# Loading S1 and S2 on GpSimd's queue, keys and v on even and odd partitions, and another order, in a polysketch attention with an ELU block behind it

## The chip, the cores and the metric

One core of one Trainium2 chip. The metric is the device time of one execution in microseconds (us): the median of the runs, lower is better. Engines are named as in the profile: PE (TensorE, with PEld for its weight loads), DVE (VectorE), ACT (ScalarE), POOL (GpSimd) and SP (SyncE, which here only issues DMAs).

## The reference

Attention without a softmax: a key or query of 32 numbers is projected by S1 and by S2 to 8 numbers each, and the 64 products of the two are its features. The result then passes a block with two weight matrices and an ELU.

```python
# q, k, v: (4, 4, 1088, 32); S1, S2: (8, 32); w_in: (128, 2048); w_out: (2048, 128)
def phi(x):
    a = np.einsum('rd,bhsd->bhsr', S1, x)
    b = np.einsum('rd,bhsd->bhsr', S2, x)
    return np.einsum('bhsi,bhsj->bhsij', a, b).reshape(*x.shape[:-1], r * r)
q_p, k_p = (phi(q), phi(k))
kv = np.einsum('bhsf,bhsd->bhfd', k_p, v)
z = np.sum(k_p, axis=2)
num = np.einsum('bhsf,bhfd->bhsd', q_p, kv)
den = np.einsum('bhsf,bhf->bhs', q_p, z)[..., None] + 1e-06
# x = num / den, reordered to (4352, 128)
h = x @ w_in
g = np.where(h > 0.0, h, alpha * (np.exp(np.minimum(h, 0.0)) - 1.0))
return (g @ w_out).astype(np.float32)
```

S1, S2, w_in and w_out arrive as 64-bit floats; the kernel rounds them to 32 bits itself, with integer steps on the two words of each number.

## The kernel before

**Tiling.** A batch b has 1088 tokens, 17 tiles (NT) of 64. Keys and values are worked on two tiles at a time: u = 0 stands for tiles 0 to 8 (KT = 9), u = 1 for tiles 9 to 16, and partitions 0 to 63 of a 128-row tile belong to u = 0, 64 to 127 to u = 1. The u = 1 half of the ninth pair has no tile and is filled with zeros (L235 for v, L237 for kT). Queries go in groups g of 8 tiles; the hidden width of 2048 goes in 8 pairs cp of two 128-blocks c.

**The head** does batch 0. `load_hd` brings keys and queries to `hd`, `load_v` brings v; `transp` (L285, on DVE) turns keys to `kT` and queries to `qT`, with the 32 numbers of each of the 4 heads on 128 partitions. S1 and S2 land in `raw_s` (L164). DVE and POOL round them: strip (L127), low (L275, POOL), floor, shift, round_s (L119, DVE), then an add into `Sx` (L279, POOL). PE multiplies `Sx` with `ident` into `sps` (L305) and DVE masks that with `bmask` into `Sab` (L308), the weights of the features. `bmask`, `zmask` and `hmask` are three reduces of `ident` on DVE (L241 to L248); `ident` is made on POOL (masks.py). `KF_first` (L345) gives the features of the keys, one matmul for each 64-token tile and half u; `KF_first_out` (L354, ACT) copies them out in two parts. `KO_first` (L419, DVE) and `KO_pool` (L327, POOL) form the products of features; `KA_first` (L436) multiplies them with v; `Z_first`, `ZC`, `Z`, `Z_out` give the sum for the denominator; `KS_copy`, `KS_turn`, `KS_out` turn kv to `kvS`. On the query side there are `q1_first` (L524), `q1z_first` (L537), `q2_out` (L624), `q4_early` (L637, transposes on PE), `q1_second` (L546), `den_wide`, `den_turn`, `den_out` (L645 to L657), and `q5_early` with `q5_early_out` (L663, L675), which writes `xg`, the x of group 0. `mm1_first` multiplies its halves with the first block of w_in.

**The weights.** `load_w` issues 256 KB pieces on SP's queue; `R1(step, i)` is one rounding step of piece i of the list `order`: low (L142), strip (L127 on DVE, L129 on ACT), floor (L132), shift (L135), round_s (L119), whole (L145, POOL). Pieces 0 and 1 are w_in of cp 0 and 1, piece 2 is w_out of cp 0, and so on. `load_rest` issues everything beyond the first two pieces; a small memset on POOL (L221), behind `KO_pool`, stands ahead of it.

**The body.** For each group and pair: `mm1` (PE, h = w_in times xg), `elu_a` (ACT, L927 and L929), `elu_d` (DVE, L935, writes gg), and the product with w_out. For group 0 that is `mm2`; `mm2_blocks` does pair 0 of group 1; later pairs use `mm2_seven`, seven products in place of eight, which also needs `sums7` on POOL (L792 to L799) and `weights7`. h has four buffers in PSUM, e two and gg three. `KF_late`, `KO`, `KA`, `queries` and so on bring in batches 1 to 3 among these.

**The order.** Nothing is scheduled by a planner at build time: each engine and queue runs its instructions in the order in which the calls stand, from `zls = {}` on, in a list of 868 calls written out one by one. SP, ACT and POOL each have a DMA queue of their own; a DMA that waits holds what stands behind it on the same engine.

```python
for x, (eng, src) in enumerate(((nc.sync, S1), (nc.scalar, S2))):   # L161
for x, src, t0, t1 in (("k", k, 0, KT), ("k", k, KT, NT), ("q", q, 0, 8)):   # L167
    for c, eng in enumerate((nc.sync, nc.scalar)):
        load_hd(eng, x, src, 0, t0, t1, slice(c, c + 1))
load_v(0, (nc.sync, nc.scalar))
```

Of the kernel before, what the change touches and what calls it, by code (L numbers as in the profile page):

```python
# [12 lines left out]
F32 = mybir.dt.float32  # L13
# [16 lines left out]
def kernel(  # L30
# [21 lines left out]
    nc = tc.nc  # L52
# [21 lines left out]
    kT = [const.tile([FD, 2 * KT, 64], F32, name=f"kT{b}") for b in range(2)] * 2  # L74
    qT = [const.tile([FD, NT, 64], F32, name=f"qT{b}") for b in range(2)] * 2
    qE = const.tile([FD, 2, 64], F32, name="qE")

# [6 lines left out]
    def load_v(b, engs=(nc.sync, nc.sync)):  # L84
        for u, eng in enumerate(engs):
            t0, t1 = u * KT, min(NT, u * KT + KT)
            r = slice(64 * u, 64 * u + 64)
            src = v[b].rearrange("h (y t) d -> y h t d", t=NT)[:, :, t0:t1, :]
            eng.dma_start(vt[b][r, :VN].rearrange("p (h t d) -> p h t d", h=H, t=KT)[:, :, :t1 - t0, :], src)
# [67 lines left out]
    S16 = const.tile([2 * R, D], F32, name="S16")  # L157
    wide = S1.dtype != F32
    if wide:
        raw_s = const.tile([2 * R, D, 2], U32, name="raw_s")  # L160
    for x, (eng, src) in enumerate(((nc.sync, S1), (nc.scalar, S2))):  # L161
        rs = slice(R * x, R * x + R)
        if wide:
            eng.dma_start(raw_s[rs].rearrange("p c w -> p (c w)"), src.bitcast(U32))  # L164
        else:
            eng.dma_start(S16[rs, :], src)
# [67 lines left out]
    for b in range(B):  # L234
        nc.gpsimd.memset(vt[b][64:, :VN].rearrange("p (h t d) -> p h t d", h=H, t=KT)[:, :, KT - 1, :], 0.0)  # L235
        if b < 2:
            nc.gpsimd.memset(kT[b][:, NT:, :], 0.0)  # L237
# [46 lines left out]
    def transp(dst, x, b, t0, t1):  # L284
        nc.vector.transpose(dst[b][:, t0:t1, :].rearrange("p t (a c) -> p c t a", c=2), hd[x, b][:, :, t0:t1, :])  # L285
# [55 lines left out]
    def KF_first(*todo):  # L341
        if not kf_ps:
            kf_ps.extend(psum.tile([P, 512], F32, name="abp", tag="h", bufs=4) for _ in range(2))
        for i, u in todo:
            nc.tensor.matmul(kf_ps[i // 5][64 * u:64 * u + 64, 64 * (i % 5):64 * (i % 5) + 64],  # L345
                             kT[0][:, u * KT + i, :], Sab[:].rearrange("p h y -> p (h y)"),
                             skip_group_check=True, tile_position=(0, 64 * u))
# [9 lines left out]
    def KF_late(b, step=None):  # L357
# [4 lines left out]
        for c in range(4):  # L362
            u, w = divmod(c, 2)
            for g2 in range(2):
# [3 lines left out]
                                 kT[b][r, u * KT:u * KT + KT, 32 * w:32 * w + 32],  # L368
# [649 lines left out]

    transp(kT, "k", 0, 2, 5)
    KF_first((0, 0), (1, 0))  # L1020
    transp(kT, "k", 0, KT, KT + 5)
    KF_first((2, 0), (3, 0), (4, 0))
    KF_first((0, 1), (1, 1), (2, 1))
    transp(kT, "k", 0, 5, KT)
    KF_first((3, 1), (5, 0))
    KF_first((4, 1), (6, 0))
    KF_first_out(0)
    transp(kT, "k", 0, KT + 5, NT)
    transp(qT, "q", 0, 0, 8)
    KF_first((5, 1), (7, 0))  # L1030
    KF_first((6, 1), (8, 0))
    KF_first((7, 1), (8, 1))
    KF_first_out(1)
    KO_pool()
    load_rest()
    KO_first(4, 5)
    KO_first(5, 7)
    keep_warm(1, 96)
    Z_first(0, 1, 2, 3, 4)
    q1_first(0, 1)  # L1040
    q1_first(2, 3)
    Z_first(5, 6, 7, 8)
    zl = ZC(0, feats["z"])
    q1_first_out()
    q2_out(0, 1)
    Z(0, feats["z"], zl)
    KO_first(7, KT)
    Z_out(0, feats["z"])
    zq = q1z_first()
    q2_out(0, 0)  # L1050
    KA_first(range(4, KT), True, False)
    q2_prod(0, zq)
    KA_first(range(4), False, True)
    make_Sxp()
    q4_early(0, 0)
    transp(qT, "q", 0, 8, 13)
    q2_sum(0)
    transp(qT, "q", 0, 13, NT)
    R1(low, 0)
    R1(strip, 0, nc.scalar)  # L1060
    q2_rec(0)
    R1(strip, 1, nc.scalar)
    q4_early(0, 1)
    R1(floor, 0)
    R1(floor, 1)
    R1(shift, 0)
    R1(shift, 1)
    R1(round_s, 0)
    KS_copy()
    KS_turn()  # L1070
    abwp = q1_second()
    den_wide()
    q4_out(0, 0)
    KS_out()
# [3 lines left out]
    R1(round_s, 1)  # L1078
    q2_prod(1)
    den_out()  # L1080
    q5_early(0)
    q5_early_out(0, 0)
    q5_early_out(0, 1)
    R1(strip, 2, nc.scalar)
    whole_half(0, 1)
    whole_half(0, 0)
    mm1_first(0, (0,))
    mm1_first(0, (1,))
    mm1_first(1, (0, 1))
    R1(low, 1, nc.gpsimd)  # L1090
    q2_sum(1)
    q2_rec(1)
    q2_an(1)
    R1(low, 3)
    R1(low, 2)
    R1(strip, 3, nc.scalar)
    R1(whole, 1)
    mm1(0, 1, (1,))
    R1(strip, 4)
    q2_out(1, 1)  # L1100
    q2_out(1, 0)
    R1(floor, 4)
    R1(low, 4)
    elu_a(0, 0, 0, (0,))
    elu_a(0, 0, 0, (1,))
    R1(floor, 2)
    R1(shift, 4)
    R1(shift, 2)
    R1(round_s, 4)
    elu_a(0, 0, 1, (0,))  # L1110
    R1(whole, 4)
    R1(round_s, 2)
    R1(whole, 2)
    q4_early(1, 1)
    q4_out(1, 1)
    q4_early(1, 0)
    q4_out(1, 0)
    mm1(0, 1, (0,))
    elu_a(0, 0, 1, (1,))
    elu_d(0, 0, 0)  # L1120
    elu_d(0, 0, 1)
    KT_out(0)
    R1(floor, 3)
    R1(strip, 5)
    R1(floor, 5)
    q5_early(1)
    elu_a(0, 1, 0, (0,))
    elu_a(0, 1, 0, (1,))
    mm1(0, 2, (0,))
    elu_a(0, 1, 1, (0,))  # L1130
    R1(strip, 7)
    R1(shift, 3)
    R1(round_s, 3)
    elu_a(0, 1, 1, (1,))
    q5_early_out(1, 0)
    q5_early_out(1, 1)
    R1(whole, 3)
# [829 lines left out]
```

## Time and profile before

| | us |
|---|---|
| median of 3 runs | 259.7 (259.54 to 260.39) |
| the profiled execution | 259.92 |
| its span, from the first to the last instruction | 258.0 |
| first DMA issue on SP and ACT | 0.74 and 0.75 |
| first matmul of mm1_first | 15.68 |
| last large products end near | 254.5 |

Times in the profile count from the start of the span. Busy time is the time in which an engine has an instruction under way; a matmul's end is modelled. Behind each group stands in brackets the idle time of its engine just before it and what ended it. A group "x4" of a timeline is four instructions of one kind in a row, and its duration runs from the start of the first to the end of the last. "SPq" and "ACTq" are the sequencers of the two engines as they issue DMAs.

### The profile page before, as it was taken

Reading aid. Unit: us, or ns where it says so; the run is one execution under the profiler, and the core shown is the slowest. Engines: PE = TensorE matmul, PEld = TensorE weight load, DVE = VectorE, ACT = ScalarE, POOL = GpSimd, SP = SyncE. Lnnn points to the kernel's source line nnn. Section 1 sums busy time; section 2 is a strip of 40 time slices with the busy share of each in tenths; the row PEclk is TensorE's granted clock in tenths of the full one; section 3 lists DMA queues with packets and bytes.
Section 4 is the critical chain, followed back from the end, with each engine's and each line's share of the span. In section 5 each row is a group of like instructions: output and inputs, shape, how many; then the busy total and the mean of one; then the engine's idle time right before and its main releaser. Section 6 shows DMA issues by size and latency. Waiting matters only on the chain.

```text
span 258.0 us, 9832 instructions
## 1 busy us (share of the span) xinstructions
PE 252.2 (98%) x4135; PEld 160.6 (62%) x4135; DVE 175.1 (68%) x342; ACT 180.4 (70%) x355; POOL 185.3 (72%) x236
## 2 busy tenths in 40 slices
PE   8889999999999999999999999999999999999994
PEld 7752332436647667577566666667666666667994
DVE  5889999699879774889377965664265445644641
ACT  2589975857677757486568757776677777777792
POOL 5533457986996877877787889879589888888310
PEclk9999999999999999999999999999999999999999
DMA  6899866032100001210002042312101100110021
GB/s 189 239 286 276 276 176 173 4 102 47 27 5 4 3 10 38 32 24 3 3 10 31 5 89 33 86 33 36 20 1 21 23 3 0 22 27 0 3 31 33
DMA packets 30427, 15.61 MB, mean 60 GB/s; under 512 B 22544, under 2 KB 28048, under 8 KB 30384
## 3 DMA queue, kind: packets, MB, share of 16 engines
q1 hardware_dynamic: 29520, 14.22, 22.9%
q10 hardware_dynamic: 800, 0.71, 1.0%
q8 instruction: 32, 0.52, 0.9%
q14 instruction: 11, 0.09, 0.1%
q0 software_dynamic: 64, 0.07, 0.1%
HBM read 11.31 MB, written 2.36 MB: 53 GB/s over the span
## 4 chain that ended last, share of the span: by engine, by line
PE 98%; DVE 0%; issue 0%; ACT 0%; DVEq 0%
PE h L259 46%; PE pb L836 18%; PE pa L836 15%; PE o L259 5%; PE ol L259 3%; PE idle L267 2%; PE kv L450 1%; PE abp L345 1%; PE qtp L637 1%; PE h L571 1%; PE h L723 1%; PE pb L812 1%; PE xps L663 1%; PE kfps L366 1%; PE kv L436 0%; PE h L735 0%
## 5 line engine op out<-in xcount | busy, mean ns | idle before, releaser
L935 DVE SCALAR_TENSOR_TENSOR gg<-e,h 128x512 f32<-128x512 f32 x128 | 85.2, 682 | 60.3 <-ACT e L929 44.6
L259 PE MATMUL h<-xg,W 128*32 128x512 f32 (+2 forms) x768 | 120.7, 584 | 0.7 <-DVE xg L675 0.7
L927 ACT ACTIVATE e<-h 128x512 f32<-128x512 f32 x128 | 74.2, 591 | 48.7 <-PE h L259 46.0
L792 POOL TENSOR_TENSOR tt<-gg 128x512 f32<-128x512 f32 x55 | 72.1, 1312 | 26.5 <-DVE gg L935 20.2
L929 ACT ACTIVATE e<-e 128x512 f32<-128x512 f32 x128 | 78.6, 630 | 2.7
L259 PEld LDWEIGHTS h<-xg,W 128*32 128x32 f32 (+1 forms) x768 | 34.4, 119 | 47.1 <-issue 32.8
L799 POOL TENSOR_TENSOR tt<-gg,tt 128x256 f32<-128x256 f32 x55 | 41.2, 753 | 3.1
L797 POOL TENSOR_TENSOR tt<-tt,gg 128x256 f32<-128x256 f32 x55 | 40.3, 735 | 3.4
L836 PEld LDWEIGHTS pa<-gg,W 128*64 128x64 f32 (+1 forms) x528 | 25.6, 125 | 24.1 <-issue 23.1
L836 PE MATMUL pa<-gg,W 128*64 128x128 f32 (+1 forms) x528 | 32.5, 273 | 0.0
L836 PE MATMUL pb<-tt,SS 128*64 128x128 f32 (+1 forms) x472 | 29.5, 273 | 0.0
L836 PE MATMUL pa<-tt,SS 128*32 128x128 f32 (+1 forms) x404 | 25.3, 273 | 0.0
L145 POOL TENSOR_TENSOR W<-W,raw 128x256 uint32<-128x256 uint32 (+2 forms) x12 | 11.9, 997 | 17.0 <-ACT e L929 7.3
L836 PEld LDWEIGHTS pb<-tt,SS 128*64 128x64 f32 (+1 forms) x472 | 22.7, 127 | 0.0
L836 PE MATMUL pb<-tt,W 128*64 128x128 f32 (+1 forms) x292 | 21.9, 273 | 0.0
L836 PE MATMUL pb<-gg,SS 128*64 128x128 f32 (+1 forms) x292 | 21.9, 273 | 0.0
L836 PEld LDWEIGHTS pa<-tt,SS 128*32 128x32 f32 (+1 forms) x404 | 17.0, 120 | 0.0
L259 PE MATMUL o<-gg,W 128*32 128x512 f32 x128 | 15.5, 593 | 0.0
L836 PEld LDWEIGHTS pb<-gg,SS 128*64 128x64 f32 (+1 forms) x292 | 13.9, 124 | 0.0
L836 PEld LDWEIGHTS pb<-tt,W 128*64 128x64 f32 (+1 forms) x292 | 13.9, 124 | 0.0
L988 DVE SCALAR_TENSOR_TENSOR gg<-e,h 128x256 f32<-128x256 f32 x16 | 6.6, 418 | 6.4 <-PE h L259 3.2
L259 PEld LDWEIGHTS o<-gg,W 128*32 128x32 f32 x128 | 4.2, 110 | 8.6 <-issue 8.2
(177 smaller groups left out, 271.8 us busy)
## 6 DMA issues: line engine op xcount, KB each, us to landing
raw<-in_moe_w_in_dram SPq DMA_DIRECT2D x8, 256.0 KB, 5.5
raw<-in_moe_w_out_dram SPq DMA_DIRECT2D x8, 256.0 KB, 4.5
out_dram<-ob SPq DMA_DIRECT2D x112, 16.0 KB, 1.5
hd_k<-in_k_dram SPq DMA_DIRECT2D x3, 544.0 KB, 4.1
hd_q<-in_q_dram SPq DMA_DIRECT2D x3, 544.0 KB, 6.0
v<-in_v_dram SPq DMA_DIRECT2D x4, 288.0 KB, 4.8
raw<-qpF SPq DMA_DIRECT2D x16, 64.0 KB, 2.0
v<-in_v_dram SPq DMA_DIRECT2D x3, 256.0 KB, 5.1
```

Of the source, the lines that this page charges most:

```text
L145: nc.gpsimd.tensor_tensor(dst.bitcast(U32), dst.bitcast(U32), words(raw)[0], op=ADD)
L259: nc.tensor.matmul(dst[c:c + tile], lhs[:, c:c + tile], rhs, skip_group_check=True, tile_position=(0, c), **kw)
L267: nc.tensor.matmul(idle[c:c + tile, :cols], ones[:, :tile], ones[:, :cols], skip_group_check=True, tile_position=(0, c))
L345: nc.tensor.matmul(kf_ps[i // 5][64 * u:64 * u + 64, 64 * (i % 5):64 * (i % 5) + 64], kT[0][:, u * KT + i, :], Sab[:].rearrange("p h y -> ...
L792: nc.gpsimd.tensor_tensor(_ap(ts[g, cp][:, 0], [[4 * P, 2], [P, 2], [1, P]]), _ap(gs[g, cp][:, 0, P:], [[4 * P, 2]] + us), _ap(gs[g, cp][: ...
L797: nc.gpsimd.tensor_tensor(t[:, 1], t[:, 2], quarter(g, cp, 0, 0), op=ADD)
L799: nc.gpsimd.tensor_tensor(t[:, 3], quarter(g, cp, 1, 0), t[:, 1], op=SUB)
L836: nc.tensor.matmul(bank[r:r + width[0], P * col:P * col + P], lhs[:, w:w + width[0]], rhs[:, u], start=(first and i in ((0,) if g == 1 els ...
L927: nc.scalar.activation(e, hs[g, cp][c][:, :n], RELU, scale=-1.0)
L929: nc.scalar.activation(e, e, EXP, scale=-1.0)
L935: nc.vector.scalar_tensor_tensor(gs[g, cp][:, c, :n], es[g, cp][:, c, :n], -1.0, hs[g, cp][c][:, :n], op0=ADD, op1=MAX)
L988: nc.vector.scalar_tensor_tensor(gs["last", k // 2][:, k % 2, :2 * P], es["last", k // 2][:, k % 2, :2 * P], -1.0, hs["last", k][:, :2 * P ...
```

## The change

S1 and S2 are loaded on POOL's queue, ahead of all other work of the kernel on POOL; SP and ACT then begin with the keys. Directly behind these two loads POOL clears the ninth pair of v of batch 0 (`clear_v`), now on all 128 partitions, ahead of `two` and `ident`; the other three stand where they stood. Rows of v go to the even partitions for u = 0 and to the odd ones for u = 1, and the columns of kT likewise (`transp` writes every fourth element of a row for keys, where it wrote every second). With that, one tile of kT holds a pair, and `KF_first` needs one matmul of 128 columns of weights where there were two of 64; `KF_late` reads the same columns from their new places. The list of calls is another one: 864 calls, the same ones except for those of `KF_first`, in another order throughout. Shown are the changes ahead of the list, and the first part of the list.

```diff
@@ -71,9 +71,24 @@
     hd = {}
 
     vt = [const.tile([P, VN], F32, name=f"v{b}") for b in range(B)]
-    kT = [const.tile([FD, 2 * KT, 64], F32, name=f"kT{b}") for b in range(2)] * 2
+    kT = [const.tile([FD, KT, P], F32, name=f"kT{b}") for b in range(2)] * 2
     qT = [const.tile([FD, NT, 64], F32, name=f"qT{b}") for b in range(2)] * 2
     qE = const.tile([FD, 2, 64], F32, name="qE")
+
+    S16 = const.tile([2 * R, D], F32, name="S16")
+    wide = S1.dtype != F32
+    if wide:
+        raw_s = const.tile([2 * R, D, 2], U32, name="raw_s")
+    for x, (eng, src) in enumerate(((nc.gpsimd, S1), (nc.gpsimd, S2))):
+        rs = slice(R * x, R * x + R)
+        if wide:
+            eng.dma_start(raw_s[rs].rearrange("p c w -> p (c w)"), src.bitcast(U32))
+        else:
+            eng.dma_start(S16[rs, :], src)
+    def clear_v(b):
+        nc.gpsimd.memset(vt[b][:, :VN].rearrange("p (h t d) -> p h t d", h=H, t=KT)[:, :, KT - 1, :], 0.0)
+
+    clear_v(0)
 
     def load_hd(eng, x, src, b, t0, t1, c=slice(0, 2)):
         if (x, b) not in hd:
@@ -84,9 +99,8 @@
     def load_v(b, engs=(nc.sync, nc.sync)):
         for u, eng in enumerate(engs):
             t0, t1 = u * KT, min(NT, u * KT + KT)
-            r = slice(64 * u, 64 * u + 64)
             src = v[b].rearrange("h (y t) d -> y h t d", t=NT)[:, :, t0:t1, :]
-            eng.dma_start(vt[b][r, :VN].rearrange("p (h t d) -> p h t d", h=H, t=KT)[:, :, :t1 - t0, :], src)
+            eng.dma_start(vt[b][u::2, :VN].rearrange("p (h t d) -> p h t d", h=H, t=KT)[:, :, :t1 - t0, :], src)
 
     idr = const.tile([P, 2 * R, R], F32, name="idr")
     nc.vector.memset(idr[:], 0.0)
@@ -154,16 +168,6 @@
 
 
 
-    S16 = const.tile([2 * R, D], F32, name="S16")
-    wide = S1.dtype != F32
-    if wide:
-        raw_s = const.tile([2 * R, D, 2], U32, name="raw_s")
-    for x, (eng, src) in enumerate(((nc.sync, S1), (nc.scalar, S2))):
-        rs = slice(R * x, R * x + R)
-        if wide:
-            eng.dma_start(raw_s[rs].rearrange("p c w -> p (c w)"), src.bitcast(U32))
-        else:
-            eng.dma_start(S16[rs, :], src)
     for x, src, t0, t1 in (("k", k, 0, KT), ("k", k, KT, NT), ("q", q, 0, 8)):
         for c, eng in enumerate((nc.sync, nc.scalar)):
             load_hd(eng, x, src, 0, t0, t1, slice(c, c + 1))
@@ -232,9 +236,10 @@
     ident = const.tile([P, P], F32, name="ident")
     make_identity(nc, ident[:])
     for b in range(B):
-        nc.gpsimd.memset(vt[b][64:, :VN].rearrange("p (h t d) -> p h t d", h=H, t=KT)[:, :, KT - 1, :], 0.0)
+        if b:
+            clear_v(b)
         if b < 2:
-            nc.gpsimd.memset(kT[b][:, NT:, :], 0.0)
+            nc.gpsimd.memset(kT[b][:, KT - 1, 1::2], 0.0)
 
 
     bmask = const.tile([FD, H], F32, name="bmask")
@@ -282,7 +287,12 @@
         nc.vector.tensor_copy(Sx[:2 * R], _ap(S16[:], [[0, H], [1, D]]))
 
     def transp(dst, x, b, t0, t1):
-        nc.vector.transpose(dst[b][:, t0:t1, :].rearrange("p t (a c) -> p c t a", c=2), hd[x, b][:, :, t0:t1, :])
+        if x == "q":
+            d = dst[b][:, t0:t1, :].rearrange("p t (a c) -> p c t a", c=2)
+        else:
+            u = t0 // KT
+            d = dst[b][:, t0 - KT * u:t1 - KT * u, :].rearrange("p t (a c u) -> p c t a u", c=2, u=2)[:, :, :, :, u]
+        nc.vector.transpose(d, hd[x, b][:, :, t0:t1, :])
 
 
     SXh = const.tile([P, FD], F32, name="SXh")
@@ -341,10 +351,9 @@
     def KF_first(*todo):
         if not kf_ps:
             kf_ps.extend(psum.tile([P, 512], F32, name="abp", tag="h", bufs=4) for _ in range(2))
-        for i, u in todo:
-            nc.tensor.matmul(kf_ps[i // 5][64 * u:64 * u + 64, 64 * (i % 5):64 * (i % 5) + 64],
-                             kT[0][:, u * KT + i, :], Sab[:].rearrange("p h y -> p (h y)"),
-                             skip_group_check=True, tile_position=(0, 64 * u))
+        for i in todo:
+            nc.tensor.matmul(kf_ps[i // 5][:, 64 * (i % 5):64 * (i % 5) + 64], kT[0][:, i, :],
+                             Sab[:].rearrange("p h y -> p (h y)"), skip_group_check=True)
 
     def KF_first_out(j):
         if 0 not in feats:
@@ -365,7 +374,7 @@
                 r = slice(64 * g2, 64 * g2 + 64)
                 nc.tensor.matmul(ps[g2][32 * c:32 * c + 32, :32 * KT],
                                  Sxp[r].rearrange("p x c r -> p (x c r)"),
-                                 kT[b][r, u * KT:u * KT + KT, 32 * w:32 * w + 32],
+                                 kT[b][r, :, 32 * c:32 * c + 32],
                                  skip_group_check=True, tile_position=(64 * g2, 32 * c))
         feats[b] = ps
 
@@ -1016,874 +1025,870 @@
 
     zls = {}
 
+    keep_warm(1, 96)
     transp(kT, "k", 0, 2, 5)
-    KF_first((0, 0), (1, 0))
     transp(kT, "k", 0, KT, KT + 5)
-    KF_first((2, 0), (3, 0), (4, 0))
-    KF_first((0, 1), (1, 1), (2, 1))
+    KF_first(0, 1, 2)
     transp(kT, "k", 0, 5, KT)
-    KF_first((3, 1), (5, 0))
-    KF_first((4, 1), (6, 0))
+    KF_first(3, 4)
     KF_first_out(0)
     transp(kT, "k", 0, KT + 5, NT)
+    KF_first(5, 6)
+    KF_first(7, 8)
+    KF_first_out(1)
     transp(qT, "q", 0, 0, 8)
-    KF_first((5, 1), (7, 0))
-    KF_first((6, 1), (8, 0))
-    KF_first((7, 1), (8, 1))
-    KF_first_out(1)
+    q1_first(0, 1)
+    Z_first(0, 1, 2, 3, 4)
+    Z_first(5, 6, 7, 8)
+    q1_first(2, 3)
+    zl = ZC(0, feats["z"])
+    q1_first_out()
+    Z(0, feats["z"], zl)
+    KO_first(4, 5)
+    KO_first(5, 7)
+    R1(low, 0)
+    R1(strip, 0, nc.scalar)
     KO_pool()
     load_rest()
-    KO_first(4, 5)
-    KO_first(5, 7)
-    keep_warm(1, 96)
-    Z_first(0, 1, 2, 3, 4)
-    q1_first(0, 1)
-    q1_first(2, 3)
-    Z_first(5, 6, 7, 8)
-    zl = ZC(0, feats["z"])
-    q1_first_out()
+    KO_first(7, KT)
+    KA_first(range(4, KT), True, False)
+    Z_out(0, feats["z"])
+    q2_out(0, 0)
+    transp(qT, "q", 0, 8, 13)
+    transp(qT, "q", 0, 13, NT)
+    R1(floor, 0)
+    zq = q1z_first()
     q2_out(0, 1)
-    Z(0, feats["z"], zl)
-    KO_first(7, KT)
-    Z_out(0, feats["z"])
-    zq = q1z_first()
-    q2_out(0, 0)
-    KA_first(range(4, KT), True, False)
+    R1(strip, 1, nc.scalar)
+    q4_early(0, 0)
+    q4_out(0, 0)
+    KA_first(range(4), False, True)
+    KS_copy()
     q2_prod(0, zq)
-    KA_first(range(4), False, True)
-    make_Sxp()
-    q4_early(0, 0)
-    transp(qT, "q", 0, 8, 13)
+    R1(floor, 1)
     q2_sum(0)
-    transp(qT, "q", 0, 13, NT)
-    R1(low, 0)
-    R1(strip, 0, nc.scalar)
+    R1(shift, 1)
     q2_rec(0)
-    R1(strip, 1, nc.scalar)
+    abwp = q1_second()
     q4_early(0, 1)
-    R1(floor, 0)
-    R1(floor, 1)
+    KS_turn()
     R1(shift, 0)
-    R1(shift, 1)
+    R1(round_s, 1)
     R1(round_s, 0)
-    KS_copy()
-    KS_turn()
-    abwp = q1_second()
+    whole_half(0, 0)
+    whole_half(0, 1)
     den_wide()
-    q4_out(0, 0)
-    KS_out()
     q4_out(0, 1)
     den_turn()
     q1_second_out(abwp)
-    R1(round_s, 1)
+    KS_out()
+    q5_early(0)
+    R1(low, 2)
     q2_prod(1)
+    q2_sum(1)
     den_out()
-    q5_early(0)
+    R1(strip, 2, nc.scalar)
     q5_early_out(0, 0)
+    mm1_first(0, (0,))
     q5_early_out(0, 1)
-    R1(strip, 2, nc.scalar)
-    whole_half(0, 1)
-    whole_half(0, 0)
-    mm1_first(0, (0,))
     mm1_first(0, (1,))
-    mm1_first(1, (0, 1))
     R1(low, 1, nc.gpsimd)
-    q2_sum(1)
+    R1(whole, 1)
     q2_rec(1)
     q2_an(1)
+    R1(strip, 4)
+    R1(floor, 2)
+    q2_out(1, 1)
+    R1(shift, 2)
+    KT_out(0)
+    q2_out(1, 0)
+    R1(round_s, 2)
     R1(low, 3)
-    R1(low, 2)
     R1(strip, 3, nc.scalar)
-    R1(whole, 1)
-    mm1(0, 1, (1,))
-    R1(strip, 4)
-    q2_out(1, 1)
-    q2_out(1, 0)
-    R1(floor, 4)
     R1(low, 4)
     elu_a(0, 0, 0, (0,))
+    R1(whole, 2)
+    mm1_first(1, (0, 1))
+    R1(floor, 3)
+    elu_a(0, 0, 1, (0,))
     elu_a(0, 0, 0, (1,))
-    R1(floor, 2)
-    R1(shift, 4)
-    R1(shift, 2)
-    R1(round_s, 4)
-    elu_a(0, 0, 1, (0,))
-    R1(whole, 4)
-    R1(round_s, 2)
-    R1(whole, 2)
-    q4_early(1, 1)
-    q4_out(1, 1)
-    q4_early(1, 0)
-    q4_out(1, 0)
+    elu_a(0, 0, 1, (1,))
     mm1(0, 1, (0,))
-    elu_a(0, 0, 1, (1,))
+    mm1(0, 1, (1,))
+    elu_a(0, 1, 1, (0,))
     elu_d(0, 0, 0)
     elu_d(0, 0, 1)
-    KT_out(0)
-    R1(floor, 3)
-    R1(strip, 5)
-    R1(floor, 5)
-    q5_early(1)
+    R1(floor, 4)
+    R1(shift, 4)
+    q4_early(1, 0)
+    q4_early(1, 1)
+    R1(round_s, 4)
+    R1(whole, 4)
+    mm2(0, 0, False, (0,))
+    R1(strip, 7)
+    elu_a(0, 1, 1, (1,))
+    q4_out(1, 0)
+    elu_d(0, 1, 1)
+    R1(shift, 3)
+    q4_out(1, 1)
     elu_a(0, 1, 0, (0,))
     elu_a(0, 1, 0, (1,))
+    mm2(0, 0, False, (1,))
+    q5_early(1)
+    q5_early_out(1, 0)
+    R1(round_s, 3)
+    R1(strip, 5)
+    mm1(0, 2, (1,))
+    elu_d(0, 1, 0)
+    q5_early_out(1, 1)
+    R1(low, 5)
+    R1(low, 7)
+    R1(floor, 5)
+    elu_a(0, 2, 1, (0,))
     mm1(0, 2, (0,))
-    elu_a(0, 1, 1, (0,))
-    R1(strip, 7)
-    R1(shift, 3)
-    R1(round_s, 3)
-    elu_a(0, 1, 1, (1,))
-    q5_early_out(1, 0)
-    q5_early_out(1, 1)
     R1(whole, 3)
-    R1(low, 7)
-    elu_a(0, 2, 0, (0,))
-    R1(low, 5)
-    mm1(0, 2, (1,))
-    mm2(0, 0, False, (0,))
-    mm2(0, 0, False, (1,))
-    elu_d(0, 1, 0)
-    elu_d(0, 1, 1)
-    R1(strip, 6)
-    elu_a(0, 2, 1, (0,))
-    R1(shift, 5)
-    R1(floor, 6)
-    R1(shift, 6)
-    R1(round_s, 5)
+    mm2(0, 1, False, (0,))
+    weights7(slice(1, 2), 0)
+    mm1(1, 0, (0,))
+    mm2(0, 1, False, (1,))
     elu_a(0, 2, 1, (1,))
     R1(floor, 7)
+    R1(shift, 5)
+    R1(strip, 6)
+    R1(shift, 7)
+    elu_a(0, 2, 0, (0,))
+    weights7(slice(1, 2), 2)
+    R1(round_s, 5)
+    R1(floor, 6)
+    mm1(1, 0, (1,))
     elu_d(0, 2, 1)
+    elu_a(0, 2, 0, (1,))
+    weights7(slice(0, 1), 0)
+    elu_d(0, 2, 0)
+    elu_a(1, 0, 0, (0,))
+    mm1(1, 1, (0,))
     R1(whole, 5)
-    elu_a(0, 2, 0, (1,))
-    elu_d(0, 2, 0)
-    R1(strip, 8)
-    mm1(1, 0, (0,))
-    mm1(1, 0, (1,))
-    R1(shift, 7)
-    mm2(0, 1, False, (0,))
-    mm2(0, 1, False, (1,))
+    make_Sxp()
     R1(low, 6)
-    elu_a(1, 0, 0, (0,))
-    elu_a(1, 0, 1, (0,))
-    mm1(1, 1, (0,))
+    mm2(0, 2, False, (0,))
+    elu_a(1, 0, 0, (1,))
+    R1(low, 8)
+    mm2(0, 2, False, (1,))
+    R1(shift, 6)
     mm1(1, 1, (1,))
     R1(round_s, 6)
+    transp(kT, "k", 1, 9, NT)
+    elu_d(1, 0, 0)
+    R1(strip, 8)
+    elu_a(1, 0, 1, (0,))
+    elu_a(1, 1, 0, (0,))
+    elu_a(1, 1, 0, (1,))
     elu_a(1, 0, 1, (1,))
-    elu_d(1, 0, 1)
-    elu_a(1, 0, 0, (1,))
-    elu_d(1, 0, 0)
     R1(whole, 6)
-    R1(floor, 8)
-    mm2(0, 2, False, (0,))
-    mm2(0, 2, False, (1,))
+    weights7(slice(0, 1), 1)
     R1(round_s, 7)
     R1(whole, 7)
-    elu_a(1, 1, 0, (0,))
+    elu_d(1, 1, 0)
+    transp(kT, "k", 1, 0, 9)
+    mm1(0, 3, (1,))
+    mm2_blocks(0, (0,))
     elu_a(1, 1, 1, (0,))
+    mm1(0, 3, (0,))
     elu_a(1, 1, 1, (1,))
+    elu_d(1, 0, 1)
+    elu_d(1, 1, 1)
+    KF_late(1, None)
+    elu_a(0, 3, 0, (0,))
+    mm1(0, 4, (0,))
+    elu_a(0, 3, 1, (0,))
+    elu_a(0, 3, 0, (1,))
...
```

## The prediction

> **What bounds the kernel now.** I read the page first, then the chain of waits, the windows, the timeline of the first 20 us, and the row of the only DMA that GpSimd issues.
>
> ```profile
> span 258.0 us, 9832 instructions
> PE 252.2 (98%) x4135; PEld 160.6 (62%) x4135; DVE 175.1 (68%) x342; ACT 180.4 (70%) x355; POOL 185.3 (72%) x236
> PE 98%; DVE 0%; issue 0%; ACT 0%; DVEq 0%
> ```
>
> PE is busy nearly always and the chain of work that ended last runs on it. The windows (start:end, length, then busy time of PE, PEld, DVE, ACT, POOL, granted clock, DMA share, GB/s) tell where it is not:
>
> ```profile
> 0.00:5.00 5.00, 4.22 (x12) 3.56 (x12) 2.45 (x14) 1.48 (x2) 2.75 (x16) 1.00 0.57 171
> 5.00:10.00 5.00, 4.28 (x78) 3.60 (x76) 3.83 (x10) 2.04 (x8) 3.14 (x7) 1.00 1.00 268
> 15.00:20.00 5.00, 4.32 (x56) 2.43 (x56) 4.82 (x15) 4.43 (x10) 1.35 (x2) 1.00 0.99 309
> 25.00:30.00 5.00, 5.00 (x52) 1.46 (x48) 4.81 (x12) 4.94 (x10) 1.64 (x2) 1.00 0.84 238
> 200.00:220.00 20.00, 20.00 (x228) 13.07 (x226) 9.75 (x18) 14.72 (x27) 16.83 (x19) 1.00 0.05 8
> ```
>
> From 20 us on PE has no idle time until the last stretch, at a granted clock of 1.00. So the time is the moment at which the first large product (mm1_first, PE h L259) begins, plus a fixed amount of PE work, plus whatever PE waits after it. The first begins here:
>
> ```profile
> 15.11 0.76 DVE L675 TENSOR_TENSOR xg<-xps,dent 128x256 f32<-128x256 f32 x2 [0.49 <-PE xps L663]
> 15.68 0.64 PE L259 MATMUL h<-xg,W 128*32 128x256 f32 x8 [0.73 <-DVE xg L675]
> ```
>
> Both orders put the same PE steps before mm1_first (features, z, queries, KA, turns, q5_early), and counted call by call the two lists hold the same steps; only KF_first is cut otherwise. So the change is worth the shift of 15.68, plus the change of what PE loses afterwards. That loss is small now: from 15.68 to 21.09 PE does four mm1_first halves (4 x 0.43, half of the 0.86 that eight 512-column matmuls take in the chain), mm1(0, 1) (2 x 0.86), eight transposes (1.02) and q5_early (0.66), together 5.12 of 5.41 us: 0.3 us lost. Later the chain's pieces stand end to end. **A gain can hardly come from behind 15.68; it must come from the head.**
>
> **The head, step by step.** The head has two branches, S (L164, then S16, Sx, sps, Sab) and the keys (hd_k, then kT):
>
> ```profile
> 0.74 0.41 SPq L164 DMA_DIRECT2D raw_s<-in_S_dram  x1
> 0.75 0.60 ACTq L164 DMA_DIRECT2D raw_s<-in_S_dram  x1
> 1.05 0.29 POOL masks.py:199 TENSOR_SCALAR_AFFINE_SELECT ident<-ident 128x128 f32<-128x128 f32 x1
> 1.38 0.29 DVE L241 TENSOR_REDUCE bmask<-ident 128x4 f32<-128x128 f32 x1 [0.23 <-POOL ident masks.py:199]
> 2.33 0.24 DVE L127 TENSOR_SCALAR S<-raw_s 16x32 uint32<-16x32 uint32 x1 [0.26 <-DMA raw_s<-in_S_dram]
> 3.46 0.45 POOL L279 TENSOR_TENSOR Sx<-S,raw_s 16x128 uint32<-16x128 uint32 x1 [0.20 <-DVE S L119]
> 4.18 0.31 DVE L285 STREAM_TRANSPOSE kT<-hd_k 128x128 f32<-128x128 f32 x1 [0.87 <-DMA hd_k<-in_k_dram]
> 4.71 0.23 DVE L308 TENSOR_TENSOR Sab<-sps,bmask 128x64 f32<-128x64 f32 x1 [0.21 <-PE sps L305]
> 4.85 1.35 DVE L285 STREAM_TRANSPOSE kT<-hd_k 128x192 f32<-128x192 f32 x4
> ```
>
> *Keys.* Without the S issues ahead of them (0.41 on SP, 0.60 on ACT) the keys start 0.48 and 0.63 us earlier, and the 0.87 us wait at 4.18 shrinks. That buys nothing by itself: Sab stands behind that one transpose in DVE's order and waits for sps, that is for S (0.21 us), and the other four transposes stand behind Sab.
>
> *S on GpSimd.* The only row of a DMA issued there is the last output:
>
> ```profile
> L1010 POOL DMA_DIRECT2D out_dram<-ol x2: 529/632/735, 250.7 to 251.4; - x2
> ```
>
> Two issues took 0.53 + 0.73 = 1.26 us of GpSimd's own time. In the changed kernel they stand first on it, with clear_v(0) (0.20, row L235) behind them, and ident comes after: its end moves from 1.34 to 1.34 + 1.46 = 2.80. The three reduces on DVE that read ident stand ahead of the strip of S and end at 2.07 now, at 3.53 then. S itself lands 1.59 after its issue now (2.33 - 0.74); the second load, issued at 1.27, would land at about 2.86, an estimate that the reduces cover. So strip moves from 2.33 to 3.53, and with it round, Sx, sps and Sab: **+1.2 us**, Sab ends near 6.14 instead of 4.94. GpSimd's other memsets up to its part of S take 1.46 from ident's end (3.05 - 1.34 less 0.25 for clear_v(0)), to 4.26, under the 4.51 at which DVE's round ends. Bounds: 0, if the issues cost GpSimd nothing, and +1.4, if both cost 0.735. I take 1.2, by the row of the same engine and kind.
>
> That row has a page against the change too. The Trainium skill's page "DMA: Bandwidth & Descriptors" (section Latency and other measured facts) puts the first byte of a GpSimd DMA at about 1 us against 0.6 us on SP and ACT, 0.4 later. By that alone, with free issues, S would land at 2.73 and Sab would be 0.4 late. The trace has no landing of a small GpSimd load.
>
> *Transposes and KF_first.* Four transposes (1.35) still follow Sab, to 7.4; writing every fourth element instead of every second has no row; I take the same 1.4 ns a column (bound: 1.67, the 288-column transposes L376 at 0.48, +0.25). KF_first is 36 matmuls in 2.31 us now, 64 ns each, and ACT waits 1.5 for it until 7.09. Then it is 18 with the full width; 64-wide and 128-wide loads are alike (L524 137 ns, L637 140 ns), so I keep 64 ns (bound: 128 ns, the transposes L637, eight in 1.02). The first ten need the transposes up to 6.85 and end at 7.5, the last eight at 8.05. KF_first_out(0) and (1) end at 8.0 and 8.45 instead of 7.5 and 7.93; the three KO_first (1.70) end at 9.85 instead of 9.25: **+0.6**. Half of Sab's delay is so won back by the halved count.
>
> *From KO_first to xg.* Now this takes 15.11 - 9.25 = 5.86. In the new order DVE does Z_out 0.19, q2_out 0.68, two transposes 0.94, two floors 0.42, product and sum 0.55, two shifts 0.50, reciprocal 0.21, two round_s 0.84, q4_out 0.68, q2_prod(1) and q2_sum(1) 0.58 ahead of xg: 5.59, without a wait, because KA for tiles 4 to 8 runs while Z_out is awaited. PE and ACT meet it there: KA, q1z, q4_early, KA, q1_second, q4_early and KS_turn (0.67+0.66+0.53+0.54+0.81+0.53+0.27) end near 13.95, then KS_out 0.27, low of weight block 2 0.55, den_out 0.59: 15.4. So **-0.2**, and mm1_first begins near 16.1: **+0.4** in sum.
>
> *Moved with it.* load_rest stands behind KO_pool on GpSimd, so SP's rest of the loads starts 0.5 later (9.62 to 10.1). Early loads (keys, q, v, two w_in) start 0.5 earlier on SP; v waits for clear_v(0), done at 2.2 when SP comes to it at 2.1, so that costs nothing, but a slower GpSimd would hold v and everything behind v on SP and ACT. Halves of v on even and odd partitions are the same bytes and the same matmuls; I cost them at nothing. keep_warm moves into the wait for the transposes, where PE is free.
>
> *Behind the head.* PE's lead, counted as PE work between a pair's last mm1 and its mm2, falls in the first stretch: pair (0, 2) 6.9 to 4.3, (1, 0) 6.9 to 4.3 and, past the part of the list shown, (0, 5) 6.7 to 4.3 us. I put 0.1 us more loss here. Against the profiled execution's own 259.92 (span 258.0 and 1.92 around it) the sum gives 260.4; it lay 0.2 above the median of the runs, 259.7, and from that the forecast is 259.7 + 0.4 + 0.1 = **260.2**.
>
> **Rivals.**
>
> *A, slower: the short leads stall PE.* Now gg of pair (0, 2) is ready 4.8 us after its mm1:
>
> ```profile
> 22.94 1.72 PE o L259 x16
> 26.46 1.29 DVE L935 SCALAR_TENSOR_TENSOR gg<-e,h 128x512 f32<-128x512 f32 x2
> ```
>
> (mm1 ends at 22.94, gg at 27.75). With a lead of 4.3 PE would wait 0.5, and at three pairs 1.5, in place of my 0.1: 261.6. For it: DVE and ACT are busy 4.8 and 4.9 of 5 us there, so a late start is not made good. Against: the bare steps (0.59, 0.63, 0.68) are 1.9, and a list may place them sooner. It decides once gg comes over 4.3 us after mm1.
>
> *B, faster: GpSimd's issues are nearly free.* Then Sab stays where it is, KF_first's gain remains (KO_first about -0.6), with the -0.2: mm1_first -0.8, and 0.1 of the lost 0.3: 258.8. Against: the 529 and 735 ns above. By the later first byte on the Trainium skill's page "DMA: Bandwidth & Descriptors" it would be 259.2.
>
> *C, slower: ACT waits for weights.* The low of block 2 now stands ahead of den_out. Its load, issued near 10.1, lands after 3.9 us (as the two now issued at 9.62), at 14.0, just under the 14.25 at which ACT comes to it. With the 5.5 of the w_in loads it would be 15.6, and mm1_first 1.3 later still: 261.5.
>
> *That the early keys do nothing* is part of the forecast.
>
> **How the numbers follow.** Forecast 0.45 (its own range 259.6 to 260.7, by the bounds 0.25 and 0.2 and KF_first's), A 0.25, C 0.12, B 0.18. 0.3% is about what a measurement of this kernel tells from no change, 0.8 us: below 258.9 is faster, above 260.5 slower. Faster: 0.11 of B and 0.02 of the rest, 0.13. Slower: 0.22 of A, 0.11 of C, 0.09 of the forecast, 0.42. The range reaches to B and past A: 258.8 to 261.8.
>
> **What would show it.** Two GpSimd DMAs near 0.74 with 0.5 us or more each, ident near 2.8, Sab near 5.9, KF_first 18 instead of 36 in about 1.2 us, KO_first ending near 9.85, mm1_first near 16.1. A shows as PE idle at o or pb between 20 and 40 us, C as ACT waiting for a raw load ahead of dent. Sab before 5.2 would prove the head wrong; a mm1_first before 15.4 the forecast.

## The result and the profile after

The changed kernel takes 266.9 us (265.8 to 268.1) against 259.7 before: ratio 1.027, 95% interval 1.021 to 1.033, slower by 7.2 us and outside the range of 258.8 to 261.8. Runs of one kernel fall into groups up to some 3 us apart here, as far as the traces show by PE's rate in the first 20 us, and the comparisons leave disturbed runs out, so a ratio need not be that of the medians.

The page of the changed kernel (third line: PE's busy share in 40 slices; fourth: the granted clock; last: the chain of waits by engine):

```profile
span 266.0 us, 9796 instructions
PE 257.0 (97%) x4117; PEld 163.8 (62%) x4117; DVE 176.4 (66%) x342; ACT 180.7 (68%) x355; POOL 185.2 (70%) x238
PE   5798999999999999999999999999999999999994
PEclk9999999999999999999999999999999999999999
PE 95%; DMA 3%; DVE 0%; SPq 0%; issue 0%; ACT 0%; DVEq 0%
```

PE has the same work but for the 18 matmuls fewer of KF_first and is no less busy later; the hole is in the first slices, and the chain now begins with DMA. The head, from the timeline (start, duration, engine, line, operation, in brackets the idle time before and its releaser):

```profile
0.74 0.88 SPq L96 DMA_DIRECT2D hd_k<-in_k_dram  x2
1.28 1.20 POOL L85 DMA_DIRECT2D raw_s<-in_S_dram  x2 [0.83 <-POOLq L1957]
2.95 0.29 POOL masks.py:199 TENSOR_SCALAR_AFFINE_SELECT ident<-ident 128x128 f32<-128x128 f32 x1
3.79 0.18 DVE L253 TENSOR_REDUCE hmask<-zmask 128x4 f32<-128x16 f32 x1
6.52 0.17 DVE L141 TENSOR_SCALAR S<-raw_s 16x32 uint32<-16x32 uint32 x1 [2.55 <-DMA raw_s<-in_S_dram]
7.96 0.60 PE L315 MATMUL sps<-ident,Sx 128*128 128x16 f32 x2 [3.54 <-POOL Sx L284]
8.61 0.23 DVE L318 TENSOR_TENSOR Sab<-sps,bmask 128x64 f32<-128x64 f32 x1 [0.98 <-PE sps L315]
8.75 1.89 DVE L295 STREAM_TRANSPOSE kT<-hd_k 128x192 f32<-128x192 f32 x4
9.88 4.10 PE L355 MATMUL abp<-Sab,kT 128*128 128x64 f32 x18 [0.32 <-DVE kT L295]
14.43 1.29 DVE L428 TENSOR_TENSOR kp<-abp,abk 128x512 f32<-128x512 f32 x2 [1.23 <-ACT abk L363]
22.86 0.76 DVE L684 TENSOR_TENSOR xg<-xps,dent 128x256 f32<-128x256 f32 x2
23.43 0.85 PE L264 MATMUL h<-xg,W 128*32 128x256 f32 x12 [0.72 <-DVE xg L684]
```

The keys are issued at 0.74, as intended. S is issued at 1.28, and DVE waits 2.55 us for it, until 6.52 instead of 2.33; Sab starts 3.9 us late (8.61 against 4.71). Then KF_first takes 4.10 us with 18 matmuls where it took 2.31 with 36: 228 ns each. mm1_first begins at 23.43 instead of 15.68, **7.75 us late; from there to the end of the span it is 242.57 us against 242.32**. All but 0.25 us of the loss is in the head. The same stretch takes 242.3 to 242.9 us in every profiled run below, so what these runs differ by lies ahead of mm1_first. The windows of the same kernel add one thing (last columns: granted clock, DMA share, GB/s):

```profile
5.00:10.00 5.00, 1.71 (x7) 1.47 (x7) 2.40 (x9) 0.27 (x1) 1.09 (x4) 1.00 0.74 250
10.00:15.00 5.00, 5.00 (x44) 4.70 (x45) 2.16 (x5) 0.80 (x2) 2.29 (x5) 1.00 0.00 0
```

Between 10 and 15 us nothing is loaded at all: load_rest stands behind KO_pool, and KO_pool waits for the features. DVE does 2.16 us of work in that stretch; before, it did 4.26.

### The profile page after: what moved, and what is told of

The parts are those of the page before. It is cut to its first block, busy times and chain, and to the rows that moved or that the text cites. A ratio compares the mean times of both kernels' runs of the same rounds, so it can differ in the third digit from the quotient of the medians.

```text
span 266.0 us, 9796 instructions
## 1 busy us (share of the span) xinstructions
PE 257.0 (97%) x4117; PEld 163.8 (62%) x4117; DVE 176.4 (66%) x342; ACT 180.7 (68%) x355; POOL 185.2 (70%) x238
## 4 chain that ended last, share of the span: by engine, by line
PE 95%; DMA 3%; DVE 0%; SPq 0%; issue 0%; ACT 0%; DVEq 0%
PE h L264 44%; PE pb L845 17%; PE pa L845 14%; PE o L264 5%; PE ol L264 3%; DMA raw<-in_moe_w_in_dram 2%; PE abp L355 2%; PE kv L459 1%; DMA hd_k<-in_k_dram 1%; PE qtp L646 1%; PE kv L445 1%; PE h L580 1%; PE h L732 1%; PE pb L821 1%; PE xps L672 1%; PE kfps L375 0%
## 5 line engine op out<-in xcount | busy, mean ns | idle before, releaser
L801 POOL TENSOR_TENSOR tt<-gg 128x512 f32<-128x512 f32 x55 | 71.0, 1292 | 27.2 <-DVE gg L944 26.7
L806 POOL TENSOR_TENSOR tt<-tt,gg 128x256 f32<-128x256 f32 x55 | 41.4, 754 | 3.0
L808 POOL TENSOR_TENSOR tt<-gg,tt 128x256 f32<-128x256 f32 x55 | 40.4, 740 | 3.0
L295 DVE STREAM_TRANSPOSE kT<-hd_k 128x512 f32<-128x512 f32 (+5 forms) x11 | 10.3, 973 | 0.0
```

The lines of the kernel that those rows point to most:

```text
L295: nc.vector.transpose(d, hd[x, b][:, :, t0:t1, :])
L801: nc.gpsimd.tensor_tensor(_ap(ts[g, cp][:, 0], [[4 * P, 2], [P, 2], [1, P]]), _ap(gs[g, cp][:, 0, P:], [[4 * P, 2]] + us), _ap(gs[g, cp][: ...
L806: nc.gpsimd.tensor_tensor(t[:, 1], t[:, 2], quarter(g, cp, 0, 0), op=ADD)
L808: nc.gpsimd.tensor_tensor(t[:, 3], quarter(g, cp, 1, 0), t[:, 1], op=SUB)
```

## The experiments

**First set: S put back, S alone moved, PE kept busy, the layout alone.** Unless said otherwise "changed" is the changed kernel, "before" the one before.

*e1_s_back*, changed:

```diff
-    for x, (eng, src) in enumerate(((nc.gpsimd, S1), (nc.gpsimd, S2))):
+    for x, (eng, src) in enumerate(((nc.sync, S1), (nc.scalar, S2))):   # ahead of the keys
```

> The changed kernel with S1 and S2 issued on SP and ACT ahead of the keys again; layout, order and clear_v stay. Theory (the late landing of S does nearly all of the loss, and PE slows down because it has nothing to do while it waits): S lands near 2.3 us as in the kernel before, Sab starts near 4.7, KF_first takes about 2 us instead of 4.1, mm1_first begins near 15.5, time 258.5 to 260.5. Rival (the layout and the other order carry a large part): KF_first stays above 3.5 us and the time stays above 262.

260.9 us (259.7 to 263.0), ratio 1.0045 (0.9999 to 1.0091). S is there at 2.38, Sab starts at 4.66, mm1_first at 16.75. With two loads put back on SP and ACT the loss is gone but for about a microsecond. The spread is wide; the profiled run shows q1_first at 88 ns a matmul (eight in 0.70) against 43 before, and the granted clock reads 0.50 from 8 to 10 us, so PE still ran slowly for a while.

*e2_s_only*, before, with the two loads of S at the head of GpSimd's queue:

```diff
+    for x, (eng, src) in enumerate(((nc.gpsimd, S1), (nc.gpsimd, S2))):   # ahead of two and ident
-    for x, (eng, src) in enumerate(((nc.sync, S1), (nc.scalar, S2))):
```

> The kernel before with only the two loads of S moved to the head of GpSimd's queue; old layout, old order. Theory: S lands near 6.5 us, Sab starts near 8.6 (+3.9), PE runs the next microseconds at half its rate, mm1_first begins near 22 to 23.5, time 265 to 267.5. Rival (it takes the new order to lose that much): only the delay of Sab is seen, 263 to 264, or less.

264.5 us (264.2 to 267.6), ratio 1.017 (1.009 to 1.025).

```profile
5.83 0.17 DVE L137 TENSOR_SCALAR S<-raw_s 16x32 uint32<-16x32 uint32 x1 [2.00 <-DMA raw_s<-in_S_dram]
7.92 0.23 DVE L308 TENSOR_TENSOR Sab<-sps,bmask 128x64 f32<-128x64 f32 x1 [1.07 <-PE sps L305]
8.43 2.88 PE L345 MATMUL abp<-Sab,kT 128*64 128x64 f32 x36
```

Sab is 3.2 us late and KF_first 0.6 longer: this move alone costs 4.8 us with the old layout and order. That is less than I expected by half a microsecond and more than the rival allowed, and 2.4 less than the whole change.

*e3_warm*, changed:

```diff
-    keep_warm(3)
+    keep_warm(11)
```

> The changed kernel with keep_warm(11) in place of keep_warm(3), so that PE is busy until S is there near 8 us. Theory (PE is slow from 9.9 to 19 us because it stood idle from 4.4 to 8.0): the 18 matmuls of KF_first take about 2 us instead of 4.1, mm1_first begins 2.5 to 4 us earlier than 23.4, time 263 to 264.5. Rival (loads of 128 columns of weights are slow in themselves, near 220 ns): KF_first stays at 4.1 us and the time at 266 to 268.

263.6 us (263.6 to 265.4). The filler runs to 8.56, and then:

```profile
8.72 0.23 DVE L318 TENSOR_TENSOR Sab<-sps,bmask 128x64 f32<-128x64 f32 x1 [1.58 <-PE sps L315]
9.99 2.22 PE L355 MATMUL abp<-Sab,kT 128*128 128x64 f32 x18 [0.80 <-DVE kT L295]
```

Sab is no earlier than in the changed kernel, yet the 18 matmuls take 2.22 in place of 4.10 us, and the kernel gains 3.3 us by medians from sixteen matmuls whose result nobody reads. **So the wide loads are not what was slow: PE ran at half its rate, and work during the wait lifts it.** The filler itself shows when it rises. The first line is the filler of the changed kernel up to 4.4 us, the other two that of this run up to 5.5 us and from 5.7 to 8.5 (busy us, mean ns of one; they overlap):

```profile
L272 PE MATMUL idle<-const-float32-1.0 128*128 128x256 f32 x6 | 2.9, 656 | 0.8 <-PEq L1957 0.8
L272 PE MATMUL idle<-const-float32-1.0 128*128 128x256 f32 x11 | 5.0, 643 | 0.8 <-PEq L1957 0.8
L272 PE MATMUL idle<-const-float32-1.0 128*128 128x256 f32 x12 | 3.0, 398 | 0.0
```

These matmuls start 0.43 us apart until 5.6 us and 0.22 apart from then on. In the changed kernel's profiled run the filler ends at 4.43, before such a rise: PE did not lose its rate in the wait, it had not reached it yet. The Trainium skill's page "TensorE: Matmul & The Clock Gate" (What's actually happening) has PE's clock at half by default, and again after an idle stretch of about 3.4 us. The slow start agrees with the first. The second is not shown here: the changed kernel stood idle for 3.54 us, but it was slow before that, and e4_s_alone below is as slow with no wait above 1.36 us.

The row of the granted clock shows 9 tenths or more in every slice of the changed kernel's run. The clock records in the traces begin only when the rate first rises, at 5.61 us here and at 19.43 in the changed kernel, and the view prints 1.00 ahead of them; there only the durations tell. A later fall it does show. This profiled run is the slowest of the four (265.4), and PE is slow again from 12.4 to 15.9 us:

```profile
12.00:14.00 2.00, 2.00 (x48) 1.71 (x51) 1.54 (x4) 0.80 (x3) 1.85 (x2) 0.61 0.00 0
```

*e6_layout*, before, with the even-odd layout and KF_first in nine:

```diff
-    kT = [const.tile([FD, 2 * KT, 64], F32, name=f"kT{b}") for b in range(2)] * 2
+    kT = [const.tile([FD, KT, P], F32, name=f"kT{b}") for b in range(2)] * 2
...
+            d = dst[b][:, t0 - KT * u:t1 - KT * u, :].rearrange("p t (a c u) -> p c t a u", c=2, u=2)[:, :, :, :, u]
```

> The kernel before with the even-odd layout of v and keys and KF_first in 9 matmuls alone; S on SP and ACT, the old order. Theory (the layout is nearly neutral): KF_first in about 2 us instead of 2.3, the four transposes of keys up to 0.5 us longer, time 259.3 to 260.2. Rival (wide loads are slow in themselves): KF_first above 3.5 us, time 261 or more.

263.2 us (260.8 to 264.5) in the six of ten runs that count in the comparison, ratio 1.0105 (1.0056 to 1.0155); the other four took 264.9 to 266.4. The time missed what I expected, the two durations did not, or hardly.

```profile
4.84 1.89 DVE L295 STREAM_TRANSPOSE kT<-hd_k 128x192 f32<-128x192 f32 x4
5.98 2.22 PE L355 MATMUL abp<-Sab,kT 128*128 128x64 f32 x18 [0.72 <-DVE kT L295]
8.66 1.12 PE L533 MATMUL abqp<-Sab,qT 128*64 128x64 f32 x16
12.22 2.15 PE L445 MATMUL kv<-kp,v 128*32 128x64 f32 x72
10.00:12.00 2.00, 1.25 (x24) 1.10 (x20) 0.79 (x2) 1.52 (x5) 1.27 (x2) 0.50 0.29 101
```

Wide loads are not slow. But the transposes that write every fourth element take 1.89 in place of 1.35 us, PE waits for them (0.72), and behind that its matmuls run slowly (1.12 against 0.69 for the queries, 2.15 against 1.21 for KA) at a granted clock of 0.50 (last line, from the windows). So PE's rate fell here without any long wait; that the 0.72 us brought the fall is argued, not shown.

**Second set: why S lands late, the order alone, and a filler.**

*e4_s_alone*, changed, with a copy ahead of the keys' loads that makes them wait for S:

```diff
+    nc.vector.tensor_copy(k0[:2 * R, :, :, 0:1].rearrange("p c t d -> p c (t d)"),
+                          _ap(raw_s[:, 0, :1].bitcast(F32), [[0, 2], [0, NT]]))
     for x, src, t0, t1 in (("k", k, 0, KT), ("k", k, KT, NT), ("q", q, 0, 8)):
```

> The changed kernel, but the loads of the keys wait until S is there (a small copy from raw_s into the keys' tile stands ahead of them), so nothing else is under way while S is loaded on GpSimd's queue. Theory (S lands late because it shares the DMA engines with the keys and queries issued just before it): landing 1.6 to 2.2 us after the issue instead of 3.4 to 4.5, S there near 3.9 us. Rival (a load on GpSimd's queue takes that long by itself): 3.4 us or more, S there near 6. The time itself says little, since everything comes later: 268 to 272.

265.5 us in one run, below what I expected. The view of raw_s, first of this kernel and then of the changed one:

```profile
L85 POOL DMA_DIRECT2D raw_s<-in_S_dram x2: 544/606/667, 1.3 to 1.9; - x2
DMA to landing us min/median/max: 1.6/1.7/1.9
```

```profile
L85 POOL DMA_DIRECT2D raw_s<-in_S_dram x2: 542/606/670, 1.3 to 1.9; - x2
DMA to landing us min/median/max: 3.4/3.9/4.5
```

The issues are alike (minimum, median and maximum in ns); with nothing else under way the same 2 KB loads land in 1.6 to 1.9 us instead of 3.4 to 4.5. It is the traffic. One run can't rank this kernel against the changed one (265.8 to 268.1). But it shows that PE needs no wait of 3.4 us to be slow: it waits 1.36 us for S and 1.10 for the keys, and KF_first takes 4.10 us all the same.

```profile
5.79 0.61 PE L318 MATMUL sps<-ident,Sx 128*128 128x16 f32 x2 [1.36 <-POOL Sx L287]
8.48 4.10 PE L358 MATMUL abp<-Sab,kT 128*128 128x64 f32 x18 [1.10 <-DVE kT L298]
```

*e5_s_behind_keys*, before, with S1 on SP and S2 on ACT behind the four loads of keys instead of ahead:

```diff
-    for x, src, t0, t1 in (("k", k, 0, KT), ("k", k, KT, NT), ("q", q, 0, 8)):
+    for x, src, t0, t1 in (("k", k, 0, KT), ("k", k, KT, NT)):   # then S, then q
```

> The kernel before with S on SP and ACT, issued behind the four loads of keys instead of ahead of them. Theory (place in the traffic counts, not the engine): S lands about with the keys or after them, 4 to 5 us instead of 2.3, Sab near 6.4 to 7.4, time 261 to 263.5. Rival (only GpSimd's queue is slow, a small load on SP or ACT passes the large ones): S by 3.5, time under 261.

263.1 us (262.9 and 263.4), ratio 1.013 (1.011 to 1.015).

```profile
4.77 0.17 DVE L127 TENSOR_SCALAR S<-raw_s 16x32 uint32<-16x32 uint32 x1 [2.69 <-DMA raw_s<-in_S_dram]
6.64 0.22 DVE L311 TENSOR_TENSOR Sab<-sps,bmask 128x64 f32<-128x64 f32 x1 [0.86 <-PE sps L308]
```

Without GpSimd, S lands after the keys too, and 2.4 us later than ahead of them; here it stands behind them in their own queues. So most of the delay is S's place in the traffic. On GpSimd's queue the rounding starts 1.1 to 1.8 us later still (5.83 and 6.52), and that is the second load: in the changed kernel's trace the first lands at 4.63, about as here, and the second, issued behind it at 1.9 and so behind the first queries, at 6.42. The Trainium skill's page "DMA: Bandwidth & Descriptors" (Queues, rings and completion order) has two rules that pull apart here: the DMA engines take turns between the queues packet by packet, by which a small load would pass large ones; and the completion write of a transfer lands only after every earlier write of that DMA engine, whatever queue it came from. The landings do not decide between them: the first load comes just behind the last keys (4.44), the second just ahead of the queries (6.59 and 6.76) that were issued before it.

*e7_order*, before with the new list of calls, KF_first in its old form:

```diff
+    keep_warm(1, 96)
     transp(kT, "k", 0, 2, 5)
...
-    q2_out(0, 1)
     Z(0, feats["z"], zl)
+    KO_first(4, 5)
```

> The kernel before with the new list of calls alone: old layout with KF_first in 18 matmuls, S on SP and ACT. Theory (order and layout are nearly neutral, the loss is in the head's S and in PE's rate): 259.2 to 260.5, mm1_first near 15.6. Rival (the new order's short leads cost PE 1 us or more behind the head): 260.8 to 262.

260.1 us (259.5 to 260.6), ratio 1.0011 (0.9998 to 1.0025). mm1_first begins at 15.92. The new order is as good as the old.

*e8_fill*, e1_s_back with a longer filler ahead of KF_first:

```diff
-    keep_warm(1, 96)
+    keep_warm(2, 256)
```

> The changed kernel with S on SP and ACT ahead of the keys (as e1_s_back), and keep_warm(2, 256) in place of keep_warm(1, 96) ahead of KF_first, which fills PE's 0.8 us of waiting for the transposes. Theory (e1 has runs near 262.8 because PE falls to half its rate in the head): the runs near 262.8 go away, median 259.5 to 260.3. Rival (the scatter has another cause): the same two groups, near 259.9 and 262.8.

260.0 us (259.6 to 260.5), ratio 1.0010 (1.0001 to 1.0020); the runs above 262 are gone. The traces fit: e1's granted clock reads 0.50 from 8 to 10 us, behind a wait of 0.83, and here, with a wait of 0.16, it reads 1.00. But in e1's set the kernel before had runs above 261 too, four of 19, and in this set none of 23, so not all of the narrowing need be the filler's. That is the change without GpSimd's queue and with PE at its full rate: no gain on the kernel before.

```profile
8.68 1.29 DVE L428 TENSOR_TENSOR kp<-abp,abk 128x512 f32<-128x512 f32 x2 [0.41 <-ACT abk L363]
15.21 0.76 DVE L684 TENSOR_TENSOR xg<-xps,dent 128x256 f32<-128x256 f32 x2 [0.26 <-PE xps L672]
15.78 3.65 PE L264 MATMUL h<-xg,W 128*32 128x256 f32 x48 [0.72 <-POOL W L153]
```

From the end of KO_first (9.97) to xg it takes 5.24 us. In the changed kernel it takes 7.14 (15.72 to 22.86).

**Third set: the two prices apart.**

*e9_cold*, before:

```diff
-    keep_warm(3)
-    keep_warm(1, 224)
```

> The kernel before without the two keep_warm calls ahead of sps; S early, old layout, old order. Theory (PE's half rate has a price of its own, with S in time): the 36 matmuls of KF_first take 2.7 to 4.5 us instead of 2.3, mm1_first begins 2 to 4 us later than 15.7, time 261.5 to 264. Rival (the rate matters only behind a late S): under 260.5.

260.7 us (260.4 to 264.2), ratio 1.0054 (1.0028 to 1.0080). KF_first takes 2.88 us and mm1_first begins at 16.39. The half rate costs time with S early too, but only 0.8 us, not 2 to 4: PE was back at its full rate by 8.8 us (the 16 matmuls of q1_first in 0.69).

*e10_late_warm*, e2_s_only:

```diff
-    keep_warm(3)
+    keep_warm(10)
```

> The kernel before with S on GpSimd's queue (as e2_s_only) and keep_warm(10) in place of keep_warm(3), so that PE is busy until S is there. Theory (late S and slow PE add up): e2 less its slow stretch of about 1 us, plus up to 0.6 for warm-up work that runs past the arrival of S: KF_first 2.3 us, time 263 to 264.2. Rival (PE's rate plays no part in e2): 264.5 or more.

263.0 us (262.6 to 263.2), ratio 1.0116 (1.0097 to 1.0134).

```profile
7.95 0.23 DVE L308 TENSOR_TENSOR Sab<-sps,bmask 128x64 f32<-128x64 f32 x1 [0.95 <-PE sps L305]
8.23 1.95 PE L345 MATMUL abp<-Sab,kT 128*64 128x64 f32 x36
```

Sab 3.24 us late, PE at its full rate, time 3.0 us longer (0.0116 x 259.9): the lateness of S goes to the end nearly one for one, and the 1.5 us between this and e2 is PE's rate.

*e11_short_warm*, before:

```diff
-    keep_warm(1, 224)
+    keep_warm(1, 96)
```

> The kernel before with keep_warm(1, 96) in place of keep_warm(1, 224) ahead of sps: Sx is there at 3.9 us and sps starts at 4.2, behind the warm-up. Theory: Sab up to 0.2 us earlier, time 259.3 to 259.7, if PE stays at its full rate. Rival (the last 0.3 us of the warm-up decide about the rate): runs near 262 appear, 260.5 or more.

260.9 us (259.2 to 261.7), ratio 1.0032 (1.0012 to 1.0051). In the profiled run sps starts at 3.95 and mm1_first at 15.00, and its span is 257.3; but eight of twelve runs are above 260.7, and none of the 23 of the kernel before in the same set. Cutting 0.3 us of filler loses more than the earlier sps brings. That PE's rate is what lengthens those runs is likely but not shown, for the profiled run is one of the short ones. None of these kernels beats the one before.

## Why the prediction was wrong

The 7.2 us, by medians: the layout and order with S early and PE busy, 0.3 (e8 260.0 against 259.7); the late S with PE busy, 3.6 (e3 263.6 less e8); PE's half rate, 3.3 (266.9 less e3). The filler of e3 itself holds sps back 0.8 us (Sx is done at 7.43, sps starts at 8.21), so some of the second share belongs to the third. In the prediction's own terms, by the profiles: Sab starts 3.90 us late where it had 1.2; from there to the end of KO_first it takes 2.57 longer where it had 0.6 less; from there to xg 1.28 longer where it had 0.2 less.

- **The step that failed: "S itself lands 1.59 after its issue now ... about 2.86, an estimate that the reduces cover".** That duration came from a load with nothing ahead of it. With the keys issued ahead of it, it took 3.4 to 4.5 us; alone on GpSimd's queue it took 1.6 to 1.9 (e4), so the traffic was missing, not the engine. Sab came 3.9 us late where I had 1.2, with a bound of 1.4: I drew the bounds from GpSimd's issue time alone and gave the landing none. The sentence in the prediction that no row shows the landing of a small GpSimd load should have widened the range.
- **GpSimd's own part** was right in kind and size: issues 1.20 (I had 1.26), ident's end 3.24 (2.80; they start at 1.28, not 0.74), hmask 3.97 (3.53). It was hidden behind the later landing.
- **The earlier keys: "That buys nothing by itself"**: right as far as it goes. But the early keys are what S waits for: e4 against the changed kernel.
- **The second step that failed: "so I keep 64 ns" for KF_first (bound 128), and "Half of Sab's delay is so won back by the halved count".** It was 228 ns. At full rate it is 123 (2.22 us for 18 in e3, e6 and e8), within the bound, but then the 18 take about as long as the 36 did (2.31 before, 1.95 at full rate in e10), and nothing is won back: with S early and PE at its rate, e8 takes 5.26 us from Sab's start to the end of KO_first against 4.54 before. The rest is PE's rate, which was not in the prediction at all. It had read the granted clock of 1.00, which the view also prints where PE runs at half rate, and moved keep_warm "into the wait" without asking what 3 us without work would do. The same cause turned "-0.2" from KO_first to xg into +1.3 (7.14 against 5.86); with PE at its rate it was -0.6 (e8).
- **The transposes, "the same 1.4 ns a column" (bound 1.67)**: 1.97 (1.89 us for 960 columns), beyond the bound.
- **"A gain can hardly come from behind 15.68", and 0.1 of loss there**: right, 0.25 us. Rival A (short leads stall PE) fell: PE waits nowhere between 24 and 60 us of the changed kernel, and the new order alone is even (e7).
- **Rival B** (issues nearly free) fell: the two issues took 1.20 us. **Rival C** (ACT waits for weights) did not arise; the weights were late, and all else was later.

The direction of the head's shift was right, its size wrong by a factor of nearly twenty (0.4 against 7.75): the landing of S in traffic and PE's rate were missing, and the gain of the halved count was not there.

## What to carry to other kernels

A small load that opens the critical path belongs ahead of the large ones in time, whatever queue it is on: the duration of a landing holds only for the traffic in which it was measured, and moving the load changes that traffic. A wait at the start costs more than its length when PE runs at half its rate behind it, so ask of each new wait how long PE will have nothing to do; read the rate from the durations of like matmuls, not from the granted clock alone. Where PE was already full, a reordering that keeps its sum of work gained nothing (e7).

## What the runs showed that I had not expected

A 2 KB load on GpSimd's queue lands 1.6 to 1.9 us after its issue alone and 3.4 to 4.5 among keys and queries. Transposes on DVE that write every fourth 4-byte element take 1.97 ns a column against 1.41 for every second one. Eight idle-filling pairs of matmuls changed a kernel of 267 us by 3.3 us. With 0.3 us less filler the runs of another spread over 2.5 us, but the kernel before spread over 3.0 in the first set by itself. PE reached its full rate at 19.43 us in the changed kernel and at 13.37 in e2, by the first clock record of each trace; why so late in the one and not in the other stays open, and so does what makes the rate fall behind a wait of under 1 us.
